# Column blocks for the first softmax, a fused norm pass and unread products in a cross-covariance attention + gated FFN kernel

## Chip, cores, metric

One core of one Trainium2 chip. The metric is the device time of one execution in microseconds (us). Beside it every run lists its span (first to last instruction) and the mean granted TensorE clock over the span (1.0 is full speed). "Median" is over the runs of one series. A ratio is the mean time of one kernel's runs over the mean time of the other's runs in the same rounds, so it is not quite the ratio of the medians quoted beside it. The series of experiments ran on different chips (8, 11, 12 and 15 in the record); each has its own runs of the kernel before beside it, and a comparison of two kernels of different series also compares two chips.

## The reference

```python
# q, k, v: (4, 6016, 256) fp32, tau = 1
qn = q / (norm(q, axis=1) + 1e-6)          # norms over the 6016 rows
kn = k / (norm(k, axis=1) + 1e-6)
a  = softmax(kn.T @ qn / tau, axis=-1)     # 256 x 256 for each of 4 batches
x  = (v @ a).reshape(24064, 256)
out = (sigmoid(x @ w_gate) * (x @ w_val)) @ w_out     # w_gate, w_val: 256 x 1536
```

## The kernel before

TensorE accumulates raw scores q'k of a batch (256 x 256) and the column sums of squares in PSUM, the memory that its products are written to; the norms scale the scores afterwards. The kernel never forms x: it folds the softmax into the weights, "gh" = (e' @ w) / row sum, 12 products of 128 x 512 for each batch (two blocks i of 128 rows, two matrices G and H, three groups fg of 512 columns). The FFN then runs from transposed v: gate and value products, sigmoid on ScalarE, multiply on VectorE, out products. A chunk is 512 rows, 12 chunks a batch; batch n+1's scores, norms, softmax and gh are laid between the products of batch n.

The first batch has nothing to hide behind: its loads (13 groups of q and k), softmax and gh are the head of the program.

```python
# head, batch 0
for g in range(last0 + 2):
    if g <= last0:
        sq[g] = (squares(q, VectorE), squares(k, VectorE if g == last0 else ScalarE))
        for u in range(nt): score(0, t0, u)
    if g >= 1:
        norm_mms(ps_n0, sq.pop(g - 1), ...)      # products of one column, q then k
norms_sqrt(0); ...; copy_s(0, 0); norms_inv(0); copy_s(0, 1)
busy(12)                 # products that nobody reads: they keep TensorE's clock up
spread_k(0)              # norms of k into all partitions
busy(10)
scale_k(0); transpose_v(0, 0, ...); exps(0); preload sigmoid table
sums(0)
for n in range(4): gh(0, n, ...)
...
# later batches, laid between the products of the batch before
psm, pss = PSUM pools of one bank each      # "m" and "s"; each holds one tile at a time
at(11 * FC + 0, sums, n)                    # both row sums side by side in one tile of psm
for i in range(12):
    at(11 * FC + min(i + 1, FC - 1), gh, n, i, *((pss, "s"), (psm, "m"))[i % 2])
```

## Time and profile before

| | kernel before |
|---|---|
| median, first series (3 runs) | 832.57 us (832.55 to 833.52) |
| median with the rounds against the changed kernel (6 runs) | 833.18 us (832.55 to 833.80) |
| the run that was profiled | 834.39 us, span 832.2, clock 0.990 |

Three stretches split the span: to T, the start of the k scaling (`x_sb` on VectorE); from T to the first out product (`ps_o`), that is the first chunk; and the rest, the body. In this profile they take 38.24, 19.62 (57.86 - 38.24) and 774.36 us (832.22 - 57.86).

```profile
57.86 0.44 PE ps_o L88 x4
```

### The profile page before, as it was taken

The page shows a single profiled execution, that of the slowest core. Times are in us where ns is not written, and L with a number is a line of the kernel's source. Part 1 is how long each engine was busy: PE and PEld are TensorE (multiplying, and loading weights), DVE is VectorE, ACT ScalarE, POOL GpSimd, SP SyncE. Part 2 cuts the span into 40 slices and gives each one's busy share as a digit, 9 for nine tenths or more (in the row PEclk, how much of TensorE's full clock was granted, in tenths as well). Part 3 has the DMA queues.
Part 4 walks back from the last instruction along what each step waited for, and adds up shares of the span by engine and source line. Part 5 has one row for each costly group of instructions (what it writes and reads, how often), then busy time and mean ns, then how long its engine had stood idle before and what let it go on. Part 6 is the DMA issues. An engine that isn't in the chain of part 4 may idle for free.

```text
span 832.2 us, 13944 instructions
## 1 busy us (share of the span) xinstructions
PE 813.7 (98%) x5303; PEld 506.3 (61%) x5314; DVE 570.1 (69%) x977; ACT 391.1 (47%) x640; POOL 83.1 (10%) x159
## 2 busy tenths in 40 slices
PE   4899999999999999999999999999999999999998
PEld 4646666666666666665566666666566566666666
DVE  2367777777667777777757777777766666666664
ACT  4464444445644444444654444444555444444442
POOL 5532100002011100000220020000000000000000
PEclk9699999999999999999999999999999999999999
DMA  9999623335765543322973464323322424322211
GB/s 210 206 205 186 120 61 75 63 63 111 152 102 109 102 92 68 61 52 66 173 139 86 87 117 81 51 67 72 63 48 66 81 51 83 70 48 69 46 35 70
DMA packets 78738, 77.18 MB, mean 93 GB/s; under 512 B 50768, under 2 KB 55632, under 8 KB 78672
## 3 DMA queue, kind: packets, MB, share of 16 engines
q0 software_dynamic: 23920, 38.81, 28.0%
q1 hardware_dynamic: 54608, 36.97, 17.5%
q8 instruction: 41, 0.67, 0.3%
q10 hardware_dynamic: 144, 0.52, 0.2%
q14 instruction: 25, 0.20, 0.1%
HBM read 78.64 MB, written 24.64 MB: 124 GB/s over the span
## 4 chain that ended last, share of the span: by engine, by line
PE 95%; DMA 3%; ACT 0%; POOL 0%; issue 0%; DVE 0%; POOLq 0%
PE ps_o L88 30%; PE ps_val L88 29%; PE ps_gate L88 29%; PE ps_s L88 4%; DMA k_sb<-in_k_dram 3%; PE ps_gh L88 2%; PE ps_n L88 0%; ACT gh_H L335 0%; PE ps_busy L88 0%; ACT e_sb L288 0%; POOL q_sb L97 0%; PE ps_rk L88 0%; PE ps_tp L352 0%; POOL k_sb L97 0%; PE ps_r L88 0%
## 5 line engine op out<-in xcount | busy, mean ns | idle before, releaser
L380 DVE TENSOR_TENSOR hT<-ps_val,g_sb 128x512 bf16<-128x512 f32 (+1 forms) x576 | 391.7, 680 | 214.6 <-ACT g_sb L379 209.4
L379 ACT ACTIVATE g_sb<-ps_gate 128x512 bf16<-128x512 f32 (+1 forms) x576 | 338.4, 588 | 387.6 <-PE ps_gate L88 380.0
L88 PE MATMUL ps_val<-vT,gh_H 128*128 128x512 bf16 (+1 forms) x1152 | 338.1, 375 | 0.3
L88 PE MATMUL ps_gate<-vT,gh_G 128*128 128x512 bf16 (+1 forms) x1152 | 337.5, 375 | 0.2
L88 PE MATMUL ps_o<-w_out_sb,hT 128*128 128x256 bf16 x2256 | 326.2, 273 | 0.0
L88 PEld LDWEIGHTS <-hT 128*128 128x128 bf16 x2256 | 220.7, 98 | 124.7
L88 PEld LDWEIGHTS <-gh_H 128*128 128x128 bf16 x1152 | 112.7, 98 | 132.2 <-ACT gh_H L335 1.5
L88 PEld LDWEIGHTS <-gh_G 128*128 128x128 bf16 x1152 | 112.5, 98 | 37.4 <-ACT gh_G L335 0.3
L106 POOL DMA_DIRECT2D v_sb<-in_v_dram x48 | 25.5, 531 | 626.9 <-DMA vT<-v_sb 513.5
L406 DVE COPY out_sb<-ps_o 128x256 f32<-128x256 f32 x188 | 77.8, 414 | 13.9 <-PE ps_o L88 13.9
L88 PE MATMUL ps_s<-k_sb,q_sb 128*128 128x256 bf16 x376 | 72.2, 294 | 13.5 <-ACT k_sb L128 6.8
L88 PEld LDWEIGHTS <-q_sb 128*128 128x128 bf16 x376 | 38.9, 104 | 21.1 <-issue 7.5
L169 DVE TENSOR_TENSOR sq<-q_sb 128x1024 bf16<-128x1024 bf16 (+3 forms) x46 | 30.3, 662 | 20.8 <-PE ps_n L88 20.8
L207 DVE TENSOR_TENSOR acc<-acc,sq 128x1024 bf16<-128x1024 bf16 (+1 forms) x66 | 44.2, 670 | 0.0
L97 POOL DMA_DIRECT2D q_sb<-in_q_dram x48 | 26.5, 553 | 15.4 <-DMA q_sb<-in_q_dram 6.5
L97 POOL DMA_DIRECT2D k_sb<-in_k_dram x48 | 26.2, 546 | 13.2 <-DMA k_sb<-in_k_dram 8.4
L169 DVE TENSOR_TENSOR sq<-k_sb 128x1024 bf16<-128x1024 bf16 (+2 forms) x34 | 22.4, 658 | 0.0
L167 ACT ACTIVATE sq<-k_sb 128x1024 bf16<-128x1024 bf16 (+1 forms) x12 | 12.2, 1021 | 15.6 <-DMA k_sb<-in_k_dram 12.7
L88 PE MATMUL ps_gh<-w_val,e_sb 128*128 128x512 bf16 x44 | 13.2, 379 | 0.2
L88 PE MATMUL ps_gh<-w_gate,e_sb 128*128 128x512 bf16 x41 | 12.8, 379 | 0.2
L88 PEld LDWEIGHTS <-e_sb 128*128 128x128 bf16 x112 | 10.2, 98 | 4.4 <-ACT e_sb L288 0.7
L379 ACT ACT_TABLE_LOAD x6 | 7.7, 1283 | 9.2 <-PE ps_gate L88 9.1
(52 smaller groups left out, 106.7 us busy)
## 6 DMA issues: line engine op xcount, KB each, us to landing
out_dram<-out_sb SPq DMA_DIRECT2D x44, 512.0 KB, 2.9
v_sb<-in_v_dram POOLq DMA_DIRECT2D x44, 256.0 KB, 3.9
q_sb<-in_q_dram POOLq DMA_DIRECT2D x43, 256.0 KB, 6.5
k_sb<-in_k_dram POOLq DMA_DIRECT2D x43, 256.0 KB, 7.2
out_dram<-out_sb SPq DMA_DIRECT2D x4, 384.0 KB, 2.5
w_gate<-in_moe_w_gate_dram POOLq DMA_DIRECT2D x3, 256.0 KB, 6.8
w_val<-in_moe_w_val_dram POOLq DMA_DIRECT2D x3, 256.0 KB, 7.4
w_out_sb<-in_moe_w_out_dram POOLq DMA_DIRECT2D x1, 768.0 KB, 12.5
```

The source lines that it names most:

```text
L88: nc.tensor.matmul(out, lhsT=lhsT, rhs=rhs, start=start, stop=stop, **kw)
L97: nc.gpsimd.dma_start(out=tl[:, :nt, :], in_=rows(src, b)[:, t0 : t0 + nt, :])
L106: nc.gpsimd.dma_start(out=v_sb[:, :nt, :], in_=rows(v, b)[:, t0 : t0 + nt, :])
L167: nc.scalar.activation(out=sq[:, :nt, :], in_=src[:, :nt, :], func=ACT.Square)
L169: engine.tensor_tensor(out=sq[:, :nt, :], in0=src[:, :nt, :], in1=src[:, :nt, :], op=ALU.mult)
L207: nc.vector.tensor_tensor(out=acc[:, :nt, :], in0=acc[:, :nt, :], in1=st[b]["sq", w][:, :nt, :], op=ALU.add)
L379: nc.scalar.activation(out=g_sb[:, :n], in_=ps_gate[:, :n], func=ACT.Sigmoid)
L380: nc.vector.tensor_tensor(out=hts[b, ci][:, f, :n], in0=ps_val[:, :n], in1=g_sb[:, :n], op=ALU.mult)
L406: nc.vector.tensor_copy(out=out_sb[:, s, :], in_=ps)
```

## The change

Intent: (1) keep TensorE's clock at full speed through the loads with products that nobody reads; (2) do the first softmax in two column blocks, so that the first gh starts after half of the exponentials; (3) make six gh before the loop instead of four, in an order that completes each third of the weights early; (4) apply both norms in one VectorE instruction, for all batches.

```diff
+    busy(40)
     for g in range(last0 + 2):
...
-                squares(0, t0, nt, 1, nc.vector if g == last0 else nc.scalar),
+            engines = (nc.vector, nc.scalar) if g < last0 else (nc.scalar, nc.vector)
...
+        if g < NT // TPC - 2:
+            busy(12)
...
-            nc.vector.tensor_tensor(out=x, in0=x, in1=s["rk"], op=ALU.mult)
+            nc.vector.scalar_tensor_tensor(out=x, in0=x, scalar=s["r"][:, j : j + 1],
+                in1=s["rk"][:, ds(i * P, P)], op0=ALU.mult, op1=ALU.mult)
...
-    gh_order = [(fg, w, i) for fg in range(NFG) for w in range(2) for i in range(CB)]
+    gh_order = [(fg, w, i) for fg in range(NFG) for i in range(CB) for w in range(2)]
...
-            nc.vector.tensor_copy(out=vT[:, : nt * CB, :], in_=ps[:, : nt * CB, :])
+            half = nt * CB // 2
+            nc.vector.tensor_copy(out=vT[:, :half, :], in_=ps[:, :half, :])
+            (nc.scalar.copy if late is None else late)(vT[:, half : nt * CB, :], ps[:, half : nt * CB, :])
...
-        at(11 * FC + 0, sums, n)
+        for i in range(CB):
+            at(11 * FC + 0, sums, n, i, *((psm, "m"), (pss, "s"))[i])
...
-            at(11 * FC + min(i + 1, FC - 1), gh, n, i, *((pss, "s"), (psm, "m"))[i % 2])
+            at(11 * FC + min(i + 1, FC - 1), gh, n, i, *((psm, "m"), (pss, "s"))[i % 2])
```

More of the change, by code (lines that the diff above doesn't have):

```diff
@@ L172, in squares, with norm_mms @@
         return sq
-    def norm_mms(ps, sqs, nt, first, last):
-        for w, sq in enumerate(sqs):
+    def norm_mms(ps, sqs, nt, first, last, order=(0, 1)):
+        for w in order:
+            sq = sqs[w]
             for u in range(nt):
@@ L182, in norm_mms @@
                         ones_bf[:, 0:1],
-                        start=(first and w == 0 and u == 0 and j == 0),
+                        start=(first and w == order[0] and u == 0 and j == 0),
                         stop=(last and u == nt - 1),
@@ L215, in norms_mm @@
         ps = psm.tile([P, CB + C], FP32, tag="m", name="ps_n")
-        norm_mms(ps, (acc_q,), TPC, True, True)
+        norm_mms(ps, (acc_q,), TPC, True, True, (0,))
         for u in range(TPC):
@@ L240, in wide_scale @@
         for j in range(CB):
-            nc.vector.tensor_tensor(
-                out=s["x"][:, j, :], in0=s["s"][:, j, :], in1=s["rk"], op=ALU.mult
+            nc.vector.scalar_tensor_tensor(
+                out=s["x"][:, j, :],
+                in0=s["s"][:, j, :],
+                scalar=s["r"][:, j : j + 1],
+                in1=s["rk"],
+                op0=ALU.mult,
+                op1=ALU.mult,
             )
@@ L276, in copy_s, with scale_k @@
         nc.vector.tensor_copy(out=s["x"][:, j, :], in_=s["s"][:, j, :])
-    def scale_k(b):
+    def scale_k(b, i):
         s = st[b]
         for j in range(CB):
-            x = s["x"][:, j, :]
-            nc.vector.tensor_tensor(out=x, in0=x, in1=s["rk"], op=ALU.mult)
-    def exps(b):
-        s = st[b]
-        s["e"] = attp.tile([P, CB, C], BF16, tag="e", name="e_sb", bufs=2)
-        for j in range(CB):
-            nc.scalar.activation(
-                out=s["e"][:, j, :],
-                in_=s["x"][:, j, :],
-                func=ACT.Exp,
-                bias=shift,
-                scale=s["r"][:, j : j + 1],
-            )
@@ L296, in sums @@
-    def sums(b):
-        s = st[b]
-        ps_r = psm.tile([P, CB], FP32, tag="m", name="ps_r")
-        for i in range(CB):
-            for j in range(CB):
-                mm(
-                    ps_r[:, i : i + 1],
-                    s["e"][:, j, ds(i * P, P)],
-                    ones_bf[:, 0:1],
-                    start=(i == 0 and j == 0),
-                    stop=(j == CB - 1),
-                    skip_group_check=True,
-                )
-        r = attp.tile([P, CB], FP32, tag="rrow", name="rrow", bufs=2)
+            x = s["x"][:, j, ds(i * P, P)]
@@ new lines, in scale_k, with exps @@
+            nc.vector.scalar_tensor_tensor(
+                out=x,
+                in0=x,
+                scalar=s["r"][:, j : j + 1],
+                in1=s["rk"][:, ds(i * P, P)],
+                op0=ALU.mult,
+                op1=ALU.mult,
+            )
+    def exps(b, i):
+        s = st[b]
+        e = attp.tile([P, CB, P], BF16, tag=f"e{i}", name=f"e_sb{i}", bufs=2)
+        nc.scalar.activation(
+            out=e, in_=s["x"][:, :, ds(i * P, P)], func=ACT.Exp, bias=shift
+        )
+        s.setdefault("e", []).append(e)
+        s.setdefault("rrow", [])
@@ L310, in sums @@
+    def sums(b, i, pl=psm, tag="m"):
+        s = st[b]
+        ps_r = pl.tile([P, 1], FP32, tag=tag, name="ps_r")
+        for j in range(CB):
+            mm(ps_r, s["e"][i][:, j, :], ones_bf[:, 0:1], j == 0, j == CB - 1)
+        r = attp.tile([P, 1], FP32, tag=f"rrow{i}", name="rrow", bufs=2)
         nc.vector.tensor_scalar(out=r, in0=ps_r, scalar1=1e-9, scalar2=None, op0=ALU.add)
         nc.vector.reciprocal(r, r)
-        s["rrow"] = r
-        s["gh"] = [
+        s["rrow"].append(r)
@@ L314, in sums, with gh_tiles @@
+    def gh_tiles(b):
+        st[b]["gh"] = [
             [ghpool.tile([P, CB, FG], BF16, tag=f"{n}{fg}", name=f"gh_{n}{fg}") for fg in range(NFG)]
@@ L316, in sums, with gh @@
         ]
-    gh_order = [(fg, w, i) for fg in range(NFG) for w in range(2) for i in range(CB)]
-    def gh(b, n, pl=None, tag=None, act=0):
+    gh_order = [(fg, w, i) for fg in range(NFG) for i in range(CB) for w in range(2)]
+    def gh(b, n, pl=None, tag=None, act=None):
         s = st[b]
@@ L326, in gh @@
                 ps,
-                s["e"][:, j, ds(i * P, P)],
+                s["e"][i][:, j, :],
                 w_sb[w][fg][:, j, :],
@@ L332, in gh @@
         dst = s["gh"][w][fg][:, i, :]
-        r = s["rrow"][:, i : i + 1]
-        if n % 2 == act:
+        r = s["rrow"][i]
+        if act if act is not None else n % 2 == 0:
             nc.scalar.activation(out=dst, in_=ps, func=ACT.Copy, scale=r)
@@ L340, with transpose_v @@
     vts = {}
-    def transpose_v(b, ci, ps=None):
+    def transpose_v(b, ci, ps=None, late=None):
         t0, nt = groups[ci]
@@ L422 @@
             t0, nt = groups0[g]
-            sq[g] = (
-                squares(0, t0, nt, 0, nc.vector),
-                squares(0, t0, nt, 1, nc.vector if g == last0 else nc.scalar),
-            )
+            engines = (nc.vector, nc.scalar) if g < last0 else (nc.scalar, nc.vector)
+            sq[g] = [squares(0, t0, nt, w, engines[w]) for w in range(2)]
             for u in range(nt):
@@ L429 @@
         if g >= 1:
-            norm_mms(ps_n0, sq.pop(g - 1), groups0[g - 1][1], g == 1, g == last0 + 1)
+            norm_mms(ps_n0, sq.pop(g - 1), groups0[g - 1][1], g == 1, g == last0 + 1, (0, 1) if g <= last0 else (1, 0))
+        if g < NT // TPC - 2:
+            busy(12)
     st[0]["n"] = ps_n0
@@ L438 @@
     spread_k(0)
-    busy(10)
-    scale_k(0)
-    transpose_v(0, 0, psv.tile([P, TPC * CB, P], BF16, tag="v", name="ps_tp"))
-    exps(0)
-    nc.scalar.preload_act_table(ACT.Sigmoid)
-    sums(0)
-    for n in range(4):
-        gh(0, n, *((psg, "g"), (psv, "v"))[n % 2], act=1)
+    busy(4)
+    scale_k(0, 0)
+    scale_k(0, 1)
+    late = []
+    transpose_v(
+        0, 0, psv.tile([P, TPC * CB, P], BF16, tag="v", name="ps_tp"), lambda *a: late.append(a)
+    )
+    exps(0, 0)
+    exps(0, 1)
+    nc.scalar.copy(*late.pop())
+    gh_tiles(0)
+    sums(0, 0)
+    gh(0, 0, psg, "g", act=False)
+    gh(0, 1, psv, "v", act=True)
+    nc.scalar.preload_act_table(ACT.Sigmoid)
+    sums(0, 1, pss, "s")
+    gh(0, 2, psg, "g", act=False)
+    gh(0, 3, psv, "v", act=False)
+    gh(0, 4, pso, "o", act=True)
+    gh(0, 5, pso, "o", act=False)
     def side_work(b):
@@ L484, in side_work @@
             (10, 0, wide_scale, n),
-            (10, 0, exps, n),
+            (10, 0, exps, n, 0),
+            (10, 0, exps, n, 1),
         ):
             side.setdefault((ci, FC + s), []).append((call[0], call[1:]))
-        at(11 * FC + 0, sums, n)
+        for i in range(CB):
+            at(11 * FC + 0, sums, n, i, *((psm, "m"), (pss, "s"))[i])
+        at(11 * FC + 0, gh_tiles, n)
         for i in range(len(gh_order)):
-            at(11 * FC + min(i + 1, FC - 1), gh, n, i, *((pss, "s"), (psm, "m"))[i % 2])
+            at(11 * FC + min(i + 1, FC - 1), gh, n, i, *((psm, "m"), (pss, "s"))[i % 2])
         return side
@@ L505 @@
                     fn(*a)
-                if (b, ci) == (0, 0) and f < len(gh_order) - 4:
-                    gh(0, 4 + f, pso, "o", act=1)
+                if (b, ci) == (0, 0) and f < len(gh_order) - 6:
+                    gh(0, 6 + f, pso, "o")
             if prev is not None and block:
```

## The prediction

> **What bounds the kernel now.** I read the page first: the engine totals, the slices, the chain that ended last.
>
> ```profile
> span 832.2 us, 13944 instructions
> PE 813.7 (98%) x5303; PEld 506.3 (61%) x5314; DVE 570.1 (69%) x977; ACT 391.1 (47%) x640; POOL 83.1 (10%) x159
> ...
> PE   4899999999999999999999999999999999999998
> PEclk9699999999999999999999999999999999999999
> ...
> PE 95%; DMA 3%; ACT 0%; POOL 0%; issue 0%; DVE 0%; POOLq 0%
> ```
>
> TensorE carries 95% of the chain, and its slices are full except the first two (20.8 us each), where the granted clock also dips. A table by stages confirms that the body has nothing to give: TensorE is busy 191.98 of 192.14 us from 57.86 on, 199.84 of 200.00 twice after that. The change removes no product of the body. So only the head counts: first batch's loads, softmax, fold of the softmax into the weights (the groups "ps_gh", 12 for each batch), and the first chunk of the FFN. Its chain of waits (start, duration, what):
>
> ```profile
> 31.65 0.04 issue
> 31.70 1.87 PE ps_s L88 x8
> 33.56 0.40 PE ps_n L88 x16
> 33.97 0.88 PE ps_s L88 x4
> 34.84 0.40 PE ps_n L88 x16
> 35.24 0.45 PE ps_s L88 x2
> 35.69 0.30 PE ps_n L88 x12
> 35.99 1.30 PE ps_busy L88 x12
> 37.29 0.92 PE ps_rk L88 x4
> ...
> 38.24 0.43 DVE x_sb L282
> ...
> 38.70 1.10 ACT e_sb L288 x2
> ...
> 47.34 0.70 ACT gh_H L335
> ```
>
> Before 31.65 this chain is the load of k: the loads set the pace until then. From 31.70 TensorE runs without a break to 38.2. Eight score products take 1.87 us here; the timeline has the same eight in 1.03 us at 29.22. So the stretch after the loads runs at half clock. The clock's own table, cut into windows of 3.41 us at the edges that I found by narrowing (17.54, 27.78, 31.2 and 38.02 us):
>
> ```profile
> 10.71:14.13 3.42, 2.26 (x38) 2.01 (x34) 1.32 (x2) 1.87 (x2) 1.59 (x3) 1.00 1.13 210
> 14.13:17.54 3.41, 1.95 (x42) 1.73 (x40) 1.20 (x2) 1.30 (x2) 1.41 (x3) 1.00 1.11 207
> ...
> 27.78:31.20 3.42, 2.24 (x44) 1.98 (x43) 1.38 (x2) 1.08 (x2) 1.76 (x3) 1.00 1.13 203
> 31.20:34.61 3.41, 2.92 (x28) 2.16 (x28) 0.43 (x2) 1.62 (x2) 2.85 (x5) 0.50 1.24 204
> 34.61:38.02 3.41, 3.41 (x48) 3.23 (x46) 1.65 (x6) 1.52 (x3) 2.27 (x4) 0.50 1.24 204
> ```
>
> First number after the width is TensorE's busy time, the third from the right its clock. A window with 2.26 us busy was followed by full clock, those with 1.95 and 2.24 by half, one with 3.41 us by full again.
>
> **What the Trainium skill says.** "TensorE: Matmul & The Clock Gate", section "What's actually happening": a free-running window of 4096 cycles (3413 ns) decides between half and full clock by how busy the array was. The trace agrees: its edges lie 10.24, 3.41 and 6.83 us apart, which are 3, 1 and 2 windows. The page counts on an idle window for throttling; here windows about two thirds busy were enough, so the measurement decides. "VectorE: DVE Perf Modes", section "The perf-mode tier table": a tensor_tensor with a PSUM operand runs at 1x. Here 256 fp32 columns take 0.42 us and 512 take 0.69, 0.27 us for 256 more, about one column a cycle at the page's 0.96 GHz. "ScalarE: Activation LUTs", section "What ACT_TABLE_LOAD costs": some 1283 ns for each load plus a drain; this trace has 1.28 us and the next ScalarE instruction 0.02 us later, so I charge 1.3.
>
> **The change, part by part.**
>
> (1) Unread products while loading: 12 after each of the first nine groups, 40 at the start. At full clock one costs 0.056 us (ten end in 0.72 us with the tail of the last), so 0.67 us a group. A group now takes 0.87 (scores) + 0.54 (norms) = 1.41 us of a period of some 2.5 us set by the loads; 1.41 + 0.67 = 2.08 still fits. No load depends on it. The gain is only the clock at the end. If it is full from 31.70:
> scores of group 10 end at 31.70 + 0.87 = 32.57, norms of group 9 at 33.11, scores of group 11 (four, 0.43) at 33.54, norms of group 10 at 34.08. Then the squares of the last group: before, VectorE made both, one after the other (0.29 each); now ScalarE makes q's (0.41, an estimate from 1.06 for 1024 columns and 0.63 for 512) from 33.93, VectorE k's from 34.18 to 34.47, since the k buffer is freed by the last norm. Scores of group 12 end at 34.30, norms of 11 (eight, 0.27) at 34.57, norms of 12 at about 34.75. Before, this point was 36.0. The norms' data are there: the last k tile lands at 27.17 + 6.5 = 33.67.
> Square root to reciprocals took 36.03 to 36.62, so 0.6 us: ready at 35.4. The twelve unread products end at 34.75 + 0.67 = 35.42. The spread of the k norms took 1.11 us at half clock, at full I estimate 0.65: scaling starts at 36.1, called T. Before, T was 38.24. Gain 2.1 us, all of it from the clock and its knock-on. At half clock the swap of the squares gives nothing: k's square still waits for the norms of group 10 and ends at 35.63 as before.
>
> (2) Softmax by column blocks. Before: two scalings of 256 columns (issued 0.375 apart), two exponentials (done T + 1.55), sums, reciprocals T + 1.87 to 2.23, first scaled gh T + 2.34 to 3.1. Now four fused scalings of 128 columns: 0.42 - 0.13 = 0.28 us each, issued about 0.24 apart. First exponential (256 elements, 0.59) T + 0.53 to 1.1, second done T + 1.6. VectorE then: scalings to T + 0.98, half of the transposed v to 1.35, reciprocal of block 0 to 1.72, gh 0 1.85 to 2.6, reciprocal of block 1 to 2.95, gh 2 to 3.8, gh 3 to 4.55 (0.75 each). ScalarE: its half of v to 2.25, gh 1 to 2.94, sigmoid table to 4.23, gh 4 to 4.94. So the first gate product is ready at T + 3.8, where before it was T + 3.6: the earlier block is spent on more VectorE work. No gain here by itself.
>
> (3) Six gh instead of four before the loop, ordered so that each third of the weights is complete early. gh 5 needs a weight that lands at 32.64 + 7.4 = 40.04, which is T + 3.9, so TensorE stands in front of it: gh 5 to T + 4.38, gate and value of step 0 to T + 5.25. After that: 11 steps of 0.865, six gh of 0.432, the transposes 0.45: 9.52 + 2.59 + 0.45 = 12.56, the chunk ends at T + 17.8. Before: it ended at 56.84, T + 18.6, and 0.31 us each was lost twice where a value product waited for ScalarE's gh of the same third (the last line of the chain above is one). These two waits go, since those gh are now made four or more steps ahead. Gain 0.8 us; at half clock, with T late and the weight already there, I get T + 17.56 and a gain of 1.0.
>
> (4) Later batches: one fused VectorE pass for both norms, exponentials without a pointer scale, two pairs of [128,1] reciprocal steps for one pair of [128,2], about 0.33 us more VectorE time for each of three batches. VectorE has 69% use and TensorE shows no wait there: 0. The score tile's bank is now held by the last gh, scaled at 242.3 to 243.05 before, and wanted at 243.36: tight but free.
>
> Sum: 2.1 + 0.8 = 2.9 us, 829.7 us.
>
> **The rivals.** (a) The clock drops anyway. In the window 27.78 to 31.2 I estimate busy time as 2.24 + 0.67 less some 0.4 of work that now falls earlier, 2.5 us: above the 2.26 that kept it. But unread products stop at about 28.8, and the window's phase may differ in another run; one from 28.8 to 32.2 would hold only 1.41 + 0.47 = 1.9 us, which was too little before. Then only (3) is left: 831.5. (b) It drops one window later, at 34.6: the twelve products and the spread run slow, 0.6 + 0.5 us lost, 830.8. (c) Weight loads take the end of the loads' place: the arrival at 40.04 already costs 0.4 us above; if transfers slip further, every us there eats a us of gain. The DMA share of over 1.0 in the table speaks for it, the unchanged order of loads against. (d) VectorE and ScalarE become the bound in the first steps, their queues being full from T to T + 5.5: up to 1 us, 830.7.
>
> **Range and chances.** I give the full clock 0.65, rival (b) 0.15, (a) 0.2: 829.7, 830.8, 831.5, mean 830.2. As (c) and (d) only cost, while the median follows the first case, I take 830.0, range 828.7 to 831.8. Two per cent is 16.65 us, twice the whole stretch from the end of the loads to the first gate product (8.2 us): faster 0.01, same 0.98, slower 0.01.
>
> **What would show each step.** Granted clock 1.00 from about 11 us through 40, scores of group 10 in about 1.03 us instead of 1.87; k scaling at about 36.1 instead of 38.24; first gate product delayed to about T + 4.4 with a wait for the value weight in front of gh 5; no ScalarE wait in the chain between 42 and 57; the first chunk's end near 54.0 instead of 56.84, and all later work moved by the same amount. I am wrong if the clock table shows 0.5 after 31 us, if loads land later than before, or if waits appear at the batch boundaries near 242, 442 and 641 us.

## The result

| | before | changed |
|---|---|---|
| median (6 runs each) | 833.18 us | 834.52 us (834.33 to 836.24) |
| ratio, 95% interval | | 1.0021 (1.0008 to 1.0034) |
| span of the profiled run | 832.2 | 833.3 |

The changed kernel is slower by 0.2%: small, but clear of the noise, and in the other direction from the forecast 830.0. (By the 2% rule that is "same", the class that the prediction gave 0.98.) The page of the changed kernel (span, engine totals, the clock row in 40 slices, the chain by engine):

```profile
span 833.3 us, 14257 instructions
PE 819.0 (98%) x5456; PEld 513.1 (62%) x5456; DVE 571.5 (69%) x987; ACT 391.2 (47%) x642; POOL 83.2 (10%) x159
...
PEclk9999999999999999999999999999999999999999
```

The dip in the first slices of the clock row is gone, but a slice is 20.8 us wide: the profile still has one window of half clock, from 33.22 to 36.63. The chain of waits in the head:

```profile
33.22 0.04 issue
33.26 1.01 PE ps_s L88 x4
34.27 0.40 PE ps_n L88 x16
...
35.42 1.30 PE ps_busy L88 x12
36.72 0.54 PE ps_rk L88 x4
...
37.28 0.61 DVE x_sb L289 x2
...
52.91 0.61 ACT g_sb L387
53.52 0.02 issue
53.55 0.70 DVE hT L388
...
56.61 0.44 PE ps_o L88 x4
```

T is 37.28 (before 38.24), and the first out product comes at 56.61 (before 57.86): the head won 1.25 us. But the whole span lost 1.11, so the body, 776.72 us against 774.36, lost 2.36. The view of waits, on TensorE alone, has one line that the kernel before does not have (engine and tile, what it waited for: total us, times, longest):

```profile
PE ps_gh L88 <- DVE rrow L314: 1.9, 3, 0.6
```

Three times, once for each later batch. The first of them in order of time (start, duration, engine, line, operation), in the changed kernel:

```profile
223.05 1.28 ACT L387 ACT_TABLE_LOAD   x1 [2.99 <-PE ps_gate L88]
...
224.32 0.60 PE L88 MATMUL ps_o<-w_out_sb,hT 128*128 128x256 bf16 x4
...
224.87 0.56 DVE L388 TENSOR_TENSOR hT<-ps_val,g_sb 128x384 bf16<-128x384 f32 x1 [1.76 <-ACT g_sb L387]
225.35 0.15 DVE L314 TENSOR_SCALAR rrow<-ps_r 128x1 f32<-128x1 f32 x1
...
225.55 0.59 PE L88 MATMUL ps_gh<-w_gate,e_sb 128*128 128x512 bf16 x2 [0.63 <-DVE rrow L314]
```

and the same place in the kernel before:

```profile
225.57 0.60 PE L88 MATMUL ps_o<-w_out_sb,hT 128*128 128x256 bf16 x4
...
226.12 0.56 DVE L380 TENSOR_TENSOR hT<-ps_val,g_sb 128x384 bf16<-128x384 f32 x1 [1.76 <-ACT g_sb L379]
226.22 0.38 PE L88 MATMUL ps_gh<-w_gate,e_sb 128*128 128x512 bf16 x1
...
226.60 0.15 DVE L310 TENSOR_SCALAR rrow<-ps_r 128x2 f32<-128x2 f32 x1
```

VectorE reads the row sums equally late in both, 1.03 us after the start of the out products: the read stands behind an hT multiply, which waits for a sigmoid, which waits for a table load. Before, gh 0 ran ahead of that read, because it wrote to the other bank: its second product starts at 226.22 (the record of the first is missing), the read at 226.60. Now it starts only after the read. The four out products at 224.32 take 0.44 us of issue, so TensorE could have gone on at 224.76 and stood until 225.55: 0.79 us, and 3 x 0.79 = 2.37, the loss of the body.

### The profile page after: what moved, and what is told of

It is laid out like the page before. It is cut to its first block, busy times and chain, and to the rows that moved or that the text cites. A ratio compares the mean times of both kernels' runs of the same rounds, so it can differ in the third digit from the quotient of the medians.

```text
span 833.3 us, 14257 instructions
## 1 busy us (share of the span) xinstructions
PE 819.0 (98%) x5456; PEld 513.1 (62%) x5456; DVE 571.5 (69%) x987; ACT 391.2 (47%) x642; POOL 83.2 (10%) x159
## 4 chain that ended last, share of the span: by engine, by line
PE 94%; DMA 3%; ACT 1%; DVE 0%; POOL 0%; issue 0%; POOLq 0%; ACTq 0%
PE ps_o L88 29%; PE ps_gate L88 29%; PE ps_val L88 29%; PE ps_s L88 4%; DMA k_sb<-in_k_dram 3%; PE ps_gh L88 2%; ACT L387 0%; PE ps_n L88 0%; DVE hT L388 0%; ACT g_sb L387 0%; POOL q_sb L97 0%; PE ps_busy L88 0%; ACT L462 0%; POOL k_sb L97 0%; ACT gh_G L341 0%
## 5 line engine op out<-in xcount | busy, mean ns | idle before, releaser
L88 PE MATMUL ps_s<-k_sb,q_sb 128*128 128x256 bf16 x376 | 66.8, 274 | 6.6 <-DMA k_sb<-in_k_dram 5.3
L88 PEld LDWEIGHTS <-q_sb 128*128 128x128 bf16 x376 | 36.7, 98 | 12.8 <-issue 6.5
L169 DVE TENSOR_TENSOR sq<-q_sb 128x1024 bf16<-128x1024 bf16 (+2 forms) x45 | 30.1, 670 | 19.1 <-PE ps_n L88 10.8
L341 ACT ACTIVATE gh_G<-ps_gh,rrow 128x512 bf16<-128x512 f32 x22 | 15.1, 687 | 14.0 <-PE ps_gh L88 14.0
L343 DVE TENSOR_SCALAR gh_H<-ps_gh,rrow 128x512 bf16<-128x512 f32 x23 | 17.0, 743 | 1.4 <-PE ps_gh L88 1.4
L88 PE MATMUL ps_busy<-ones_bf 128*128 128x128 bf16 x164 | 13.7, 248 | 1.1 <-DVE shift L125 1.1
```

What stands on the lines that cost most here:

```text
L88: nc.tensor.matmul(out, lhsT=lhsT, rhs=rhs, start=start, stop=stop, **kw)
L169: engine.tensor_tensor(out=sq[:, :nt, :], in0=src[:, :nt, :], in1=src[:, :nt, :], op=ALU.mult)
L341: nc.scalar.activation(out=dst, in_=ps, func=ACT.Copy, scale=r)
L343: nc.vector.tensor_scalar(out=dst, in0=ps, scalar1=r, scalar2=None, op0=ALU.mult)
```

## The experiments

Theory A: the loss is the PSUM banks. The row sums of a later batch are unread in both small banks when gh 0 needs one. Rival B: it is the longer VectorE list of the later batches (fused pass, one more pair of reciprocal steps). For the head: why did the clock give so little, and what is the new ScalarE wait at 52.91? The three stretches of each profile, read off its chain and its timeline, with the spans and clocks of all runs (the profiled one first):

| kernel | T | T to first out | body | spans of the runs | clock of the runs |
|---|---|---|---|---|---|
| before | 38.24 | 19.62 | 774.36 | 36 runs: 829.8 to 832.2, mean 830.8 | 0.987 to 0.994 |
| changed | 37.28 | 19.33 | 776.72 | 833.3 834.3 832.4 832.5 832.7 832.5 | 0.997 0.996 1.0 0.999 1.0 0.999 |
| one bank | 36.09 | 19.50 | 774.34 | 829.9 830.5 831.9 830.6 830.4 | 1.0 1.0 0.995 1.0 1.0 |
| before, two banks | 36.29 | 19.63 | 776.72 | 832.6 833.8 833.6 834.4 833.6 | 0.988 to 0.992 |
| one copy | 36.64 | 18.63 | 776.70 | 832.0 831.9 832.0 832.1 833.5 | 1.0 1.0 1.0 0.998 0.996 |
| no unread | 37.26 | 19.33 | 776.71 | 833.3 834.3 833.3 832.8 832.1 | 0.988 to 0.992 |
| to the end | 36.94 | 19.33 | 776.70 | 833.0 832.7 832.9 832.9 832.9 | 0.998 to 1.0 |
| bank and copy | 38.40 | 18.82 | 774.34 | 831.6 829.6 829.4 829.6 829.2 | 0.996 1.0 1.0 1.0 0.998 |
| before, unread | 36.34 | 19.62 | 774.36 | 830.3 830.4 831.7 831.3 831.3 | 0.997 to 1.0 |
| blocks only | 36.60 | 18.63 | 774.34 | 829.6 830.4 829.1 830.4 829.6 | 0.989 to 0.992 |
| one more | 36.61 | 18.63 | 774.36 | 829.6 829.7 829.6 829.8 829.9 | 0.999 to 1.0 |
| no swap | 36.43 | 18.62 | 774.35 | 829.4 829.5 829.4 829.6 829.7 | 0.998 to 1.0 |

(The 36 runs of the kernel before are those beside the four series of experiments.) The body takes only two values, 774.35 and 776.71, whatever came earlier. T scatters.

### One bank: the row sums side by side again

```diff
-        for i in range(CB):
-            at(11 * FC + 0, sums, n, i, *((psm, "m"), (pss, "s"))[i])
+        at(11 * FC + 0, sums_pair, n)      # both blocks' sums in one psm tile of two columns,
+                                           # then add and reciprocal for each block
...
-            at(11 * FC + min(i + 1, FC - 1), gh, n, i, *((psm, "m"), (pss, "s"))[i % 2])
+            at(11 * FC + min(i + 1, FC - 1), gh, n, i, *((pss, "s"), (psm, "m"))[i % 2])
```

> The changed kernel, but the two column sums of a later batch go side by side into one PSUM bank again, and the first gh product into the other bank; all the VectorE work of the change stays. Theory A (banks): both small banks hold unread sums, so the first gh product of each later batch waits about 0.78 us for VectorE, 3 x 0.78 = 2.35 us: without it this run is 2.3 us under the changed kernel, about 832.2, some 1 us under the kernel before, and no wait of a gh product for rrow is left at 225, 425 and 626 us. Rival B (work): the longer VectorE list of the later batches (one more pair of reciprocal steps, the fused pass) delays it, so this run stays at 834.5 and a wait stays at those places.

Measured: 832.44 us median against 832.64 of before, ratio 1.0000 (0.9987 to 1.0012); body 774.34. Its chain at the same place (the row sums are read no earlier than before):

```profile
223.46 0.44 PE ps_o L88 x4
223.90 0.05 issue
223.95 0.38 PE ps_gh L88
```

The out products are followed by gh at once. The whole 2.36 us came back with all the VectorE work still there. A holds, B falls. This run also shows the weight load that the prediction named: with T at 36.09, TensorE waited 0.3 us for the value weight in front of gh 5 (0.4 was forecast), which is why its first chunk took 19.50.

### Before, two banks: the bank part of the change alone

```diff
-        at(11 * FC + 0, sums, n)
+        at(11 * FC + 0, sums, n, ((psm, "m"), (pss, "s")))   # one tile in each bank
...
-gh, n, i, *((pss, "s"), (psm, "m"))[i % 2])
+gh, n, i, *((psm, "m"), (pss, "s"))[i % 2])
```

> The kernel before with only the banks of the change in later batches: its two column sums in two PSUM banks, the gh products starting with the first of them; separate scalings, one reciprocal, old order of gh. Theory A: three stalls of some 0.7 to 0.8 us come in, 2.1 to 2.4 us over the kernel before, about 835.4. Rival B: as the VectorE work is that of before but for one [128,1] step, within 0.3 us of the kernel before.

Measured: 835.69 us, ratio 1.0038 (1.0025 to 1.0052), body 776.72. Put into the kernel before, the two banks alone make the same 2.36 us (the means differ by 2.9, of which the scatter of T is the rest). This is the reverse of the run above, and it settles A.

### One copy: the second transposed chunk on VectorE alone

```diff
-            half = nt * CB // 2
+            half = nt * CB if late is None else nt * CB // 2
...
-            (nc.scalar.copy if late is None else late)(vT[:, half : nt * CB, :], ...)
+            if late is not None:
+                late(vT[:, half : nt * CB, :], ps[:, half : nt * CB, :])
```

> The changed kernel, but the second transposed chunk of v is copied by VectorE alone, as before; the first chunk stays split. Theory: ScalarE's half waits for VectorE's half of the same tile and holds up the sigmoid behind it, which cost TensorE 0.70 us in steps 9 to 11 of the first chunk; so 0.4 to 0.7 us under the changed kernel, about 833.9, steps of 0.86 us there. Rival: VectorE's full queue is what is late, a longer copy makes it worse, and the run is at or above 834.5.

Measured: 833.92 us, ratio to before 1.0019 (1.0007 to 1.0032); T to the first out product 18.63 instead of 19.33. In the changed kernel, ScalarE had this row (the bracket gives its idle time and what ended it):

```profile
52.43 0.59 ACT L363 COPY vT<-ps_tp 128x512 bf16<-128x512 bf16 x1 [1.09 <-DVE vT L362]
```

ScalarE stood 1.09 us until VectorE had copied its half, and the sigmoids queued behind. The two halves are written to one SBUF tile (`vT`) and read from one PSUM tile (`ps_tp`); which of the two made ScalarE wait, no run separates. With one copier the chain there holds no ScalarE and no VectorE piece, only products:

```profile
51.81 0.43 PE ps_gate L88 x2
52.24 0.43 PE ps_val L88 x2
52.67 0.43 PE ps_gate L88 x2
```

So the split copy cost 0.70 us in the second chunk. The rival (VectorE's queue is the late one) falls: giving it the longer copy helped.

### No unread products during the loads

```diff
-    busy(40)
-        if g < NT // TPC - 2:
-            busy(12)
```

> The changed kernel without the unread products while loading (40 at the start, 12 after each of nine groups); those around the spread of the norms stay. Theory (clock): the clock falls to half before the loads end, as in the kernel before, the k scaling starts near 38.2 instead of 37.3 and the run is 1 to 2 us over the changed kernel, about 835.5 to 836.5. Rival: the products give nothing, as the clock falls at 33.4 in the changed kernel too: same time within 0.5 us.

Measured: 835.24 us, mean span 833.16 against 832.95 of the changed kernel, and T 37.26 against 37.28 in the two profiles. The medians lie 0.7 us apart, outside the rival's 0.5 and short of the theory's 1 to 2; the means of time and of span lie 0.2 apart, within the scatter of both (the runs of the two kernels come from different rounds). So this is nearer the rival: the products raised the mean clock from about 0.99 to nearly 1.0 and gave some 0.2 us. The two profiles alone decide nothing, as both have half clock behind the loads (31.40 to 34.81 here, 33.22 to 36.63 there).

### Before, unread: these products alone

```diff
+    busy(40)
...
+        if g < NT // TPC - 2:
+            busy(12)
```

> The kernel before with the unread products alone. Theory (most runs of the kernel before already have the full clock after the loads, the profiled one being a slow one): the mean clock rises from 0.99 to 0.997 or more, but the median falls by 0.5 us at most, to about 832.2, and what goes is the runs above 833.5. Rival (as predicted: the clock is worth 2.1 us in a usual run): about 830.7.

Measured: 833.41 us against 832.88 of before, ratio 1.0005 (0.9991 to 1.0018). No gain; the slow end did not go either (833.87). T was 36.34 here and 36.29 in the two-bank run without any such products. T = 38.24, from which the prediction took its 2.1 us, was the late end of the scatter: its span of 832.2 is as long as the longest of the 36 of the kernel before. With 774.36 + 19.62 taken off, their mean of 830.8 leaves T at about 36.8.

What sets T once the clock is full? In the one-copy run, at full clock from 4 us on, TensorE waits for the k of group 11:

```profile
33.38 0.60 PE L88 MATMUL ps_s<-k_sb,q_sb 128*128 128x256 bf16 x4 [0.43 <-DMA k_sb<-in_k_dram]
```

T is 36.64 there. In "one more" and "no swap" the same wait is 0.42 and 0.21 us and T 36.61 and 36.43; in "one bank" these scores start at 32.92 without a wait, and T is 36.09. So with a full clock the loads are what comes next, and a usual run of the kernel before was already within some 0.5 us of that.

### Blocks only: both repairs, no unread products

> The kernel of both repairs without the unread products, so the softmax by column blocks, the order of gh and the fused pass alone against the kernel before. Theory: from the start of the k scaling to the first out product it takes 18.6 us instead of the 19.6 of the kernel before, whatever the clock did earlier, and 774.35 us after that; median 1.0 us under the kernel before, about 831.7. Rival: the column blocks give nothing and the time is that of the kernel before within 0.3 us.

(The two diffs above, and the removal of the unread products.) Measured: 831.56 us, ratio 0.9986 (0.9973 to 0.9998); T to the first out product 18.63, as expected 1.0 us below the kernel before. Why half clock during the loads costs so little, from its table by stages:

```profile
24.00:28.00 4.00, 3.80 (x32) 2.79 (x32) 1.01 (x2) 2.11 (x2) 1.63 (x4) 0.50 1.12 209
28.00:31.60 3.60, 3.13 (x44) 2.35 (x43) 1.25 (x2) 1.18 (x2) 1.90 (x3) 0.50 1.16 202
31.60:33.40 1.80, 1.80 (x23) 1.38 (x22) 0.14 (x1) 0.94 (x1) 1.73 (x3) 0.61 1.24 210
33.40:36.80 3.40, 3.29 (x66) 2.98 (x63) 1.91 (x7) 2.46 (x4) 3.04 (x5) 1.00 1.23 203
```

At half clock (0.50) the same work fills the period between two loads, 3.80 of 4.00 us, and TensorE keeps up with the loads anyway; the clock was back at full for the last groups, where it counts. That was this run's phase of the clock windows, not the kernel's doing: in the profile of "no unread" the half clock lasted to 34.81, and T was 37.26.

### Bank and copy: both repairs, unread products as in the change

> The changed kernel with both repairs: sums side by side in one bank, and the second chunk of v copied by VectorE alone. Theory: the two gains add, 2.3 + 0.5 us under the changed kernel, about 831.9, first out product near 55.1 and 774.35 us from there to the end at full clock, 0.7 to 0.9 us under the kernel before. Rival: they share a cause and only 2.3 us come, 832.4, level with the kernel before.

Measured: 831.50 us, ratio 0.9986 (0.9974 to 0.9999). The two repairs add. Four runs had spans of 829.2 to 829.6; the profiled one had 831.6:

```profile
31.60:33.40 1.80, 1.41 (x24) 1.25 (x24) 0.38 (x1) 1.06 (x1) 1.36 (x2) 0.96 1.21 198
33.40:36.80 3.40, 3.21 (x46) 2.81 (x45) 1.56 (x4) 2.04 (x4) 3.00 (x6) 0.50 1.23 206
36.80:40.00 3.20, 3.09 (x22) 2.36 (x20) 1.94 (x8) 1.42 (x3) 1.63 (x4) 0.50 1.24 205
```

Full clock up to 33, half from there to 40: the clock fell in the very stretch that it was to be kept for, some 4.4 us after the last unread products (28.8). T was 38.40.

### To the end: twelve more behind two more groups

```diff
-        if g < NT // TPC - 2:
+        if g < last0 - 1:
```

> The changed kernel, but the unread products follow two more groups (after each of the first eleven). Theory (clock by windows): in two of six runs of the changed kernel the mean clock fell to 0.997 or less and the span grew by 1 to 2 us, since a window behind the last products was too empty; with products to the end no run falls below 0.999, so no run is above 834.8, but 12 more products stand in front of the last scores and cost up to 0.5 us: median about 834.7. Rival (the stop two groups from the end was right): the products delay the last groups by over 1 us in every run, median 835.5 or more.

Measured: 834.83 us (834.69 to 835.01), clocks 0.998 to 1.0. The spans lie within 0.3 us, as the theory has it, and in the profiled run the clock held through the head. Two of its bounds were missed: two runs are at 0.998 instead of 0.999 or more (one window of 3.41 us at half clock in 833 us is worth 0.002; where it lay was not recorded), and four of the five are above its 834.8, the highest at 835.01. The price also shows: a piece of 0.69 us of unread products now stands in the chain in front of group 11's scores, and T is 36.94 where the one-copy run had 36.64.

### One more: both repairs, ten groups instead of nine

```diff
-        if g < NT // TPC - 2:
+        if g < NT // TPC - 1:
```

> Both repairs, and the unread products follow one more group (ten instead of nine): these twelve fall into the wait for group 10's data (30.6 to 31.7 us), so they stand in front of nothing. Theory (the window behind the last products decides): no run below a mean clock of 0.998, and no run like the one of 833.5; median 831.4 as in the good runs of the kernel with both repairs (831.2 to 831.5), all five within 0.6 us. Rival (the clock at the end is chance, whatever stands before it): a run with 0.996 or less and over 832.5 among the five, or a median above 831.8, as the products hold up group 10.

Measured: spans of 829.6 to 829.9, clocks 0.999 to 1.0: these twelve stand in the wait for group 10's data, the clock held in all five runs, and T was not delayed. The median, 832.51, missed the expected 831.4 and lies above the rival's mark of 831.8, and the five times spread over 0.8 us instead of 0.6. The spans say that the products are not the reason: in this series the time was 2.1 to 3.1 us over the span, where 1.9 to 2.2 is usual (why is not known). Ratio 0.9992 (0.9978 to 1.0006). By mean span the kernels with ten, nine and no groups of unread products (829.72, 829.88, 829.82) are level: ten groups narrow the scatter and do not move the mean. Spans of 0.9 us or more above the lowest of their kernel came in 8 of the 26 runs with nine groups (changed, one bank, one copy, bank and copy, before unread), and in none of the 15 with more.

### No swap: the last squares both on VectorE again

```diff
-            engines = (nc.vector, nc.scalar) if g < last0 else (nc.scalar, nc.vector)
+            engines = (nc.vector, nc.scalar if g < last0 else nc.vector)
```

> The kernel with both repairs and ten groups of unread products, but the last group's two squares both on VectorE and the norms in the order q, k, as before the change. Theory (ScalarE's 0.42 us square, behind its 0.63 us one, holds the last norms up, where VectorE took 0.29): from the start of group 11's scores to the end of the reciprocal 2.25 us instead of 2.41, spans 0.15 us shorter, about 829.55. Rival (the swap helps, as predicted for the full clock, 0.2 us or more): spans of 829.9 or more.

(On top of the kernel with ten groups; the norm products go back to the order q, k too.) Measured: 831.60 us, ratio 0.9982 (0.9968 to 0.9996), spans 829.4 to 829.7. The last square of q in the run with the swap, then without:

```profile
34.15 0.42 ACT L167 ACTIVATE sq<-q_sb 128x256 bf16<-128x256 bf16 x1
```

```profile
34.13 0.29 DVE L169 TENSOR_TENSOR sq<-q_sb 128x256 bf16<-128x256 bf16 x1 [0.76 <-PE ps_n L88]
```

From the start of group 11's scores to the end of the reciprocal: 33.34 to 35.75 with the swap (2.41 us), 33.32 to 35.56 without (2.24). The size is as expected, the reason mostly not: the square root after the last norm starts 0.06 us earlier (1.65 instead of 1.71 us after the scores), and the other 0.11 is VectorE's add of 1e-6, which took 0.28 us with the swap and 0.17 without; in "one bank", also with the swap, it took 0.17. So about 0.06 us is the swap's. The mean span fell by 0.20 us, on another chip. With T at 36.43 the chain already runs through the value weight of gh 5 (it lands at 40.10), so a still earlier T would gain nothing by itself. This is the fastest of the kernels tried, 0.2% under the kernel before.

Left open: the phase of the clock windows, which is not in the program's hands. A run at half clock behind the last products was not forced, only met. What a window needs was not tested by a run of its own, but the kept traces show more than the prediction read from one. Busy time does not order the windows; two of the changed kernel, the first followed by full clock, the second by half:

```profile
12.73:16.15 3.42, 2.14 (x37) 1.93 (x36) 0.70 (x2) 1.06 (x1) 1.07 (x3) 1.00 1.13 211
29.81:33.22 3.41, 2.21 (x44) 1.95 (x43) 1.02 (x2) 1.56 (x2) 2.37 (x4) 1.00 1.23 201
```

What orders them is the number of columns that TensorE streamed. A score product counts 256, an unread one 128, a gate, value or gh product 512, a norm product only 1, although 16 of these keep TensorE busy for 0.4 us (the fp32 spread is counted threefold, as its four products take 0.70 us against some 0.22 for four unread ones). The first window above has about 3,600 columns, the second about 2,680. From the first clock record to 45 us the twelve profiles have 138 windows of 3.41 us: every one with 3,054 columns or fewer was followed by half clock, every one with 3,100 or more by full. The counts are estimates, since some matmul records are missing and starts are rounded, and the rule is read off these traces only. It would explain the unread products: twelve of them add 1,536 columns to a window that has one or two groups' scores, 2,048 each.

## Why the prediction was wrong, step by step

| step | forecast | profiled pair | over all runs |
|---|---|---|---|
| (1) T, by the clock | -2.1 | -0.96 | near 0 |
| (2), (3) T to first out product | -0.8 | -0.29 | -0.29 |
| (4) later batches | 0 | +2.36 | +2.36 |
| sum | -2.9 | +1.11 | +2.1 (mean spans 832.95 and 830.8) |

**Step (4) failed, and turned the sign.** The prediction put the later batches at 0, by VectorE's use and the absence of waits in the kernel before, and checked one end of a bank's use (the score tile wanted at 243.36; that was indeed free). It did not check the other: who frees the bank that gh 0 writes. It named waits near 242, 442 and 641 us as a sign of being wrong; they came at the row sums, at 225, 425 and 626. The change from one sum tile to two is a bookkeeping detail of the block form, but gh 0 ran ahead of the row sums only because a free bank stood beside them. Two runs, one that takes the detail out and one that puts it in alone, each move the body by 2.36 us. The Trainium skill, "PSUM — Partial Sum Buffer", section "PSUM bank collisions raise a hardware error", asks for guards on PSUM by bank and quadrant. The wait seen here fits that but does not test it: the gh product needs no row sum itself, but its 128 x 512 fp32 output fills the bank and overwrites the sum, so a guard by address would have held it too.

**Step (1) was sized on one run.** The windows of 3.41 us are as told, and so is what half clock does (eight score products take 1.87 us instead of 1.03). At full clock T came at 36.09 in one profile, against 36.1 forecast, and at 36.43 to 36.94 in four others of the changed head, where the k of group 11 came later or unread products stood in front of it. The measure was wrong: busy time does not decide a window (see "Left open"), and the prediction's own table has one with 2.92 us (31.20, at half clock) that was followed by half again. But the 38.24 it was compared with belongs to a run of 834.39 us whose kernel had a median of 832.57, as its own times showed. Over all runs T without unread products averages about 36.8. Rival (a), the clock falling after the products stop, occurred at 33.22 in the profiled run (0.35 was given to (a) and (b) together; two of six runs had the low clock). Within the step, the swap of the last squares was put at a gain in the full clock; the kernel without it was 0.17 us faster in the profiles, of which some 0.06 us is the swap's.

**Step (2) was right.** "The first gate product is ready at T + 3.8": it started at 41.18, T + 3.9. The fused scaling was undersized: 0.34 us for 128 columns instead of 0.28, so the first exponential began at T + 0.64 instead of T + 0.53.

**Step (3) was right in what it removes and missed what it adds.** The two waits of 0.31 us for ScalarE's gh are gone, and with one copier the stretch is 18.63 us, 1.0 under the kernel before (0.8 to 1.0 forecast). The split copy in the second chunk, which the prediction took for free in its 0.45 us of transposes, gave 0.70 of that back. Rival (c), the weight load in front of gh 5, was real but small (0.3 us, and only with T near 36.1). Rival (d) shows at the start: gh 6 waits for ScalarE's gh 4 behind the sigmoid table and starts at 42.35, T + 5.07, where the forecast had gh 4 done at T + 4.94 and TensorE busy to T + 5.25.

## What to carry to other kernels

When a change splits one small tile into two, list for each bank who must have read it before the next writer starts: a product that needs no result can still wait for the bank of one. Before sizing a gain from a profile, set the profiled run's own time beside the median of the timed runs; here it was 1.8 us off, nearly the 2.1 us forecast for that stretch. And giving half of one tile to a second engine only helps if that engine need not wait until the first has done its half.

## What the Trainium skill lacked or had wrong

- "TensorE: Matmul & The Clock Gate" (section "What's actually happening") names an idle window as what lowers the clock. Here windows with TensorE busy for 2.21 us (29.81 to 33.22, changed kernel), 1.95 and 2.24 us (kernel before) of 3.41 were followed by half clock, others with 2.14 (12.73 to 16.15, changed kernel) and 2.26 by full clock. A partly busy window is enough, and the page gives no share; by streamed columns the 138 windows of the twelve profiles part between 3,054 and 3,100.
- The same page advises keeping TensorE busy; it does not say that filling stops paying once the filler ends before the critical stretch: the clock fell at about 33 us, some 4.4 us after the last unread products, in two profiles.
- "VectorE: DVE Perf Modes" (section "The perf-mode tier table") has no row for scalar_tensor_tensor. With one fp32 operand in PSUM, 128 columns took 0.34 us and four of them 1.12 us; a tensor_tensor of 256 columns took 0.42.
- "ScalarE: Activation LUTs" (section "What ACT_TABLE_LOAD costs") adds a drain of about 1.38 us to the 1.28 us of a table load. In the changed kernel the load at 40.31 took 1.28 us and the next ScalarE instruction began at 41.61, 0.02 us after it; the same held in the kernel before.
- No page that I read treats two engines writing halves of one SBUF tile; here ScalarE's copy began only as VectorE's half was done, with 1.09 us of idle time put down to it. Both also read one PSUM tile, so the guards by bank cited above would explain it as well.
